# Two score evictions, the state products and the order of transfers in the first chunk of a gated linear attention with a mixture of experts

## The chip, the cores and the metric

The kernel runs on one core of one Trainium2 chip. A core has TensorE (PE in the profile; it multiplies matrices and writes only to PSUM, 8 banks of 128 x 512 float32), VectorE (DVE), ScalarE (ACT), GpSimd (POOL) and SyncE (SP, which here only issues transfers), and 16 DMA engines that all queues share. Each engine works through its own instruction list in order; semaphores order the engines among each other. The metric is device time in microseconds (us), lower is better.

## The reference

There are 4 batches, 8 heads, 768 positions and 48 features a head. A recurrence with a gate for each feature runs over the positions, and its output goes through a mixture of four experts:

```
f = 1 / (1 + exp(-f_logit))
for t in range(S):
    state = f[:, :, t, :, None] * state + einsum('bhd,bhe->bhde', k[:, :, t], v[:, :, t])
    y[:, :, t] = einsum('bhd,bhde->bhe', q[:, :, t], state)

x = y, as (batch * position) x (head * feature)            # 3072 x 384
p = domain_probs / (sum(domain_probs) + 1e-9)
for e in range(4):
    out += p[:, e] * (relu(x @ w1[e]) @ w2[e])             # 384 -> 1024 -> 384
```

## The kernel before

**Chunks.** The 768 positions are cut into 6 chunks of 128. Within a chunk the recurrence becomes matrix products. With g = ln(1 + exp(-f_logit)) (`gate1`, `gate2`, L326 to L336) and its running sum cs, made by a product with a triangle of ones (`pe_cs`), q is multiplied by exp(-cs) and k by exp(cs) (`exps`, `expq`, `product`). Both are transposed (`pe_tp` with TensorE in chunk 0, otherwise by a transfer) into QK, the scores k.q are made (`pe_at`, L430), evicted from PSUM to AT as bfloat16 with a multiplication by a 0/1 triangle, `mask01` (`ev_at`, L433), and multiplied by v (`pe_y`, L444). From the second chunk on, the state of the chunks before is added to y (L440). After a chunk, the state takes up k'v (`pe_kv` on TensorE, L450; `ev_kv` adds it on DVE, L457) and is multiplied by the chunk's total decay (`state` on GpSimd, L462 and L465). y is then copied, transposed (`pe_xt`, L469) and copied again to become x, or is scaled and transposed by a transfer, and goes into the experts.

**Experts.** Chunks 0 and half of chunk 1 run the plain form: `mm_h` (L478) for x @ w1, a relu eviction (L489), `mm_o` (L493) for h @ w2. The rest uses a form with seven instead of eight products for a pair of experts and a pair of tiles, on scaled x: `mm_hs` (L510), relu (L516, L518), sums of blocks (`s_sum`, L528), products `mm_p` (L547) and their additions (`ev_p`, L555).

**Chunk 0.** It comes first, batch by batch (0 to 3), while all data is still on its way. f and q of chunk 0 are loaded so that two neighbouring positions stand together in one partition's run ("paired", `PAIRED = "fq"`, L291), so the running sum for q (`pe_cq`, L356) and the columns of the scores come in an order of pairs that `pe_at` undoes when it reads q: its moving operand is read as position pair by pair, with the two members a long step apart (L428), and the scores stand in the order of positions. `pe_cs` of chunk 0 also makes the total decay: eight matmuls, each with one column of `par` (L349). f, k and q are loaded by SyncE in the order of their due times; v (chunk 0) and the weights are loaded by GpSimd's queue, with a conversion to bfloat16, in the order `SEQ` ("v0 v1 w0 v2 v3 w1") and then w2 to w10. Pieces w0 and w1 are the two halves of expert 0's w1, w2 and w3 those of expert 1's, w4 and w5 the two halves of expert 0's w2; later pieces are whole matrices. `GATE` holds v0's issue until k of batch 1 has landed, and v1's until k of batch 2 has. GpSimd's eight DMA semaphores are reused in turn: an issue waits until the transfer eight issues before has landed.

**The order of the work.** No loop of the text sets the order on the engines. Every step (an `Op`, made by `P.add`) has an estimated cost for each engine that may run it, dependences, buffers that it takes and frees, and a due time ("prio"). `Plan.run` plays the program through: whenever an engine is free, it gets the ready step with the lowest due time. The list of steps in the order of the played time is then emitted, each engine's in that order. `MOVES` holds corrections for single steps: `name=offset` is added to the due time, `@ENGINE` fixes the engine. Names are `kind chunk.batch...`, for example `ev_at0 0.1` (evict scores, head half 0, chunk 0, batch 1), `kv 0.0` (state product), `h 0.0.4.0` (chunk 0, expert 0, blocks 4 to 7 of the hidden layer, columns from 0 on), `ld k0.1` (load). Steps of DMA queues are played with an estimate too, so an offset on "w 0" or "ld v0.0" changes only what the plan believes of the landing. Before the first L478 matmul, gaps that the plan sees on TensorE are filled with matmuls on a constant ("fillers", L925, 128 x 512): one for each 0.42 us before 7 us, and one for each 0.25 us after it (L914).

**State products of chunk 0.** `kv 0.b` depends on y of its batch and on the last x of chunk 0 (L715), so that all four come after the transposes of batch 3.

Of the kernel before, what the change touches and what calls it, by code (L numbers as in the profile page):

```python
# [10 lines left out]
AF = mybir.ActivationFunctionType  # L11
ALU = mybir.AluOpType
# [128 lines left out]
def kernel(  # L141
# [14 lines left out]
    T = 128  # L156
# [181 lines left out]
    def pe_cs(c, b):  # L338
# [8 lines left out]
        for i in range(NP):  # L347
            for j in range(2):
                nc.tensor.matmul(out=cs[:, HD + i:HD + i + 1], lhsT=flat(g, j * 2 + i % 2), rhs=par[:, i // 2:i // 2 + 1],  # L349
                                 start=(j == 0), stop=(j == 1), skip_group_check=True)  # L350
# [16 lines left out]
    def exps(c, b):  # L367
        cs = tl("cs", c, b)
        src = cs[:, 0:HD].rearrange("t (i r d) -> t i r d", r=2, d=D)
        for j in range(2 if c else 0):  # L370
            o, i = e_part(c, b, j), src
            if j == 0:
                o, i = (x.rearrange("t i r d -> t r i d") for x in (o, i))
            nc.scalar.activation(out=o, in_=i, func=AF.Exp, scale=1.0 if j else -1.0)  # L374
        if c == 0:
            nc.scalar.activation(out=tl("e", c, b)[:, 2 * NP * P2:], in_=cs[:, 0:HD], func=AF.Exp, scale=1.0)
            nc.scalar.activation(out=tl("egs", c, b)[0:MP, 0:NP], in_=cs[0:MP, HD:HD + NP], func=AF.Exp, scale=-1.0)
# [7 lines left out]
    def product(c, b, j, eng):  # L385
        if (c, j) == (0, 0):
# [583 lines left out]
```

## Time and profile before

| | us |
|---|---|
| runs shown | 288.28, 289.12, 294.09 (median 289.12) |
| profiled execution, its own time | 287.92 |
| its span, first to last instruction | 286.2 |
| TensorE busy | 279.5 (98%) |
| VectorE busy | 199.8 (70%) |
| ScalarE busy | 177.9 (62%) |
| GpSimd busy | 110.7 (39%) |
| L510 (x @ w1, second form) | 106.8 |
| L547 (products of the second form) | 29.0, 28.4, 28.2 and 14.7 by operands |
| L493 (h @ w2, first form) | 35.0 |
| L478 (x @ w1, first form) | 35.0 |
| L433 (masked score evictions, 48) | 30.4 |

Busy time of a group is the union of its instructions' durations. A matmul's duration includes its passage through the array, so that matmuls overlap, and the distance from start to start is what one costs in a row of them. "Idle before" is the time in which the engine did nothing ahead of an instruction, with what ended it. The granted clock of TensorE is a share of full speed. In the lines of a timeline the first number is the start in us from the first instruction, the second the duration of the run of instructions that the line merges. Data movement is dense over the first 45 us (the page's row of 40 slices shows 6 to 9 tenths there) because the weights are still coming.

### The profile page before, as it was taken

How to read it: one execution, taken by the hardware profiler on the slowest of the kernel's cores; microseconds unless marked ns; L12 is line 12 of the kernel's file. 1: busy time of each engine (PE TensorE's matmuls, PEld its weight loads, DVE VectorE, ACT ScalarE, POOL GpSimd, SP SyncE). 2: the span in 40 equal slices, each digit the busy share in tenths (PEclk: the TensorE clock that was granted, in tenths of full speed). 3: DMA queues.
4: the chain of work that ended last, by engine and by line, in shares of the span. 5: the costliest groups of instructions: out<-in, count | busy, mean ns of one | idle time of the engine just before them, and what ended most of it. 6: DMA issues, size and time to landing. Idle time of an engine off the chain costs nothing.

```text
span 286.2 us, 7542 instructions
## 1 busy us (share of the span) xinstructions
PE 279.5 (98%) x3046; PEld 237.1 (83%) x3046; DVE 199.8 (70%) x397; ACT 177.9 (62%) x334; POOL 110.7 (39%) x183
## 2 busy tenths in 40 slices
PE   5999999999999999999999999999999999999995
PEld 2768555567777999999999999999999999999995
DVE  5675123688889878987789877878682888453374
ACT  5968673558757874953577846649466667255530
POOL 5766501327773752867037276427235000000000
PEclk9999999999999999999999999999999999999999
DMA  6999999996997999899979999789744136110001
GB/s 157 213 193 207 206 192 205 190 187 141 192 166 148 210 140 236 156 168 209 214 141 186 147 212 205 142 176 187 128 55 82 30 76 123 57 60 0 30 27 57
DMA packets 153687, 41.87 MB, mean 146 GB/s; under 512 B 144028, under 2 KB 152860, under 8 KB 153652
## 3 DMA queue, kind: packets, MB, share of 16 engines
q1 hardware_dynamic: 142404, 34.66, 62.9%
q0 software_dynamic: 11248, 6.72, 16.6%
q8 instruction: 24, 0.39, 0.6%
q14 instruction: 11, 0.09, 0.1%
HBM read 31.51 MB, written 4.72 MB: 127 GB/s over the span
## 4 chain that ended last, share of the span: by engine, by line
PE 94%; SPq 2%; DMA 1%; DVE 1%; ACT 1%; issue 0%; DVEq 0%
PE ps_m L510 33%; PE ps_m L547 29%; PE ps_m L493 11%; PE ps_m L478 11%; PE ps_m L430 3%; PE ps_m L444 2%; SPq L293 1%; PE ps_m L440 1%; DMA q<-in_q_dram 1%; PE ps_m L450 1%; PE ps_m L341 1%; SPq L295 1%; PE ps_m L399 1%; PE ps_m L925 0%; DVE qk L387 0%; PE ps_m L469 0%
## 5 line engine op out<-in xcount | busy, mean ns | idle before, releaser
L510 PE MATMUL ps_m<-x,w_sb 128*128 128x256 bf16 x864 | 106.8, 273 | 0.0
L518 ACT ACTIVATE h<-ps_m 128x512 bf16<-128x512 f32 x108 | 64.3, 597 | 48.6 <-PE ps_m L510 37.8
L510 PEld LDWEIGHTS <-w_sb 128*128 128x128 bf16 x864 | 82.7, 98 | 9.2
L547 PEld LDWEIGHTS <-S 128*128 128x128 bf16 x576 | 48.8, 98 | 1.2 <-issue 0.2
L555 DVE TENSOR_TENSOR o<-ps_m,o 128x192 f32<-128x192 f32 x91 | 30.8, 352 | 23.8 <-PE ps_m L547 22.7
L547 PEld LDWEIGHTS <-h 128*128 128x128 bf16 x432 | 36.4, 98 | 0.7
L465 POOL TENSOR_TENSOR Sf<-Sf,egs 48x192 f32<-48x192 f32 x40 | 21.5, 540 | 36.1 <-DVE Sf L457 27.7
L493 PE MATMUL ps_m<-w_sb,h 128*128 128x384 bf16 x192 | 35.0, 326 | 0.0
L478 PE MATMUL ps_m<-x,w_sb 128*128 128x128 bf16 (+2 forms) x264 | 35.0, 282 | 0.0
L528 DVE TENSOR_TENSOR S<-h 128x1024 bf16<-128x1024 bf16 x36 | 28.1, 792 | 8.0 <-ACT h L518 7.9
L489 ACT ACTIVATE h<-ps_m 128x512 bf16<-128x512 f32 (+1 forms) x50 | 24.7, 508 | 13.6 <-PE ps_m L478 12.6
L433 DVE TENSOR_TENSOR AT<-ps_m,mask 128x512 bf16<-128x512 f32 x48 | 30.4, 682 | 2.7 <-PE ps_m L430 2.7
L516 DVE TENSOR_SCALAR h<-ps_m 128x512 bf16<-128x512 f32 x36 | 24.6, 688 | 10.6 <-PE ps_m L510 8.4
L478 PEld LDWEIGHTS <-w_sb 128*128 128x128 bf16 x264 | 21.8, 98 | 9.4
L413 ACT ACTIVATE yb<-ps_m,pn 128x384 bf16<-128x384 f32 x48 | 25.9, 580 | 5.6 <-PE ps_m L444 2.5
L547 PE MATMUL ps_m<-ts_sb,S 128*128 128x192 bf16 x288 | 29.0, 246 | 0.0
L547 PE MATMUL ps_m<-w_sb,S 128*128 128x192 bf16 x288 | 28.4, 246 | 0.0
L390 POOL TENSOR_TENSOR qk<-q,e 128x384 bf16<-128x384 f32 x18 | 22.4, 1251 | 15.2 <-ACT e L374 14.3
L374 ACT ACTIVATE e<-ps_m 128x384 f32<-128x384 f32 x40 | 23.1, 704 | 8.2 <-PE ps_m L341 7.2
L547 PE MATMUL ps_m<-w_sb,h 128*128 128x192 bf16 x288 | 28.2, 246 | 0.0
L493 PEld LDWEIGHTS <-h 128*128 128x128 bf16 x192 | 18.3, 98 | 11.7
L390 POOL TENSOR_TENSOR qk<-k,e 128x384 bf16<-128x384 f32 x18 | 17.9, 999 | 11.6 <-PE ps_m L444 3.6
(83 smaller groups left out, 314.9 us busy)
## 6 DMA issues: line engine op xcount, KB each, us to landing
out_dram<-o SPq DMA_DIRECT2D x23, 192.0 KB, 2.2
w_sb<-in_moe_w_dram POOLq DMA_DIRECT2D x5, 768.0 KB, 17.0
k<-in_k_dram SPq DMA_DIRECT2D x10, 384.0 KB, 4.9
q<-in_q_dram SPq DMA_DIRECT2D x10, 384.0 KB, 5.6
v<-in_v_dram SPq DMA_DIRECT2D x10, 384.0 KB, 4.5
f<-in_f_logit_dram SPq DMA_DIRECT2D x9, 384.0 KB, 5.2
w_sb<-in_moe_w_dram POOLq DMA_DIRECT2D x6, 384.0 KB, 10.1
f<-in_f_logit_dram SPq DMA_DIRECT2D x6, 192.0 KB, 3.8
```

Of the source, the lines that this page charges most:

```text
L390: return engines[eng].tensor_tensor(out=tl("qk", c, b)[:, j, :, 0:D].rearrange("t (i r) d -> t i r d", r=2), in0=tl("qk"[j], c, b // 2)[:, ...
L413: nc.scalar.activation(out=ys, in_=y, func=AF.Copy, scale=pe)
L433: nc.vector.tensor_tensor(out=tl("AT", c, b)[:, r].rearrange("s i t -> s (i t)"), in0=tl("A", c, b, r).rearrange("s i t -> s (i t)"), in1= ...
L478: nc.tensor.matmul(out=hp(c, e, fc, n0, n1, nf)[:, f], lhsT=w1_sb[:, e, kk, (fc + f) * 128:(fc + f + 1) * 128], rhs=tl("xT", c)[:, kk, n0: ...
L489: nc.scalar.activation(out=dst, in_=src, func=AF.Relu)
L493: nc.tensor.matmul(out=tl("op", c, e, nt, part)[:, cols], lhsT=tl("h", c, e, half_of(c, nt * T))[:, fc, nt * T:(nt + 1) * T], rhs=w2_sb[:, ...
L510: nc.tensor.matmul(out=out_[:, f], lhsT=w1_sb[:, e, kk, (fc + f) * 128:(fc + f + 1) * 128], rhs=tl("xs", c, hf, p)[:, el, kk, :], start=(k ...
L516: nc.vector.tensor_relu(out=dst, in_=tl("hp", c, hf, p, el, fc))
L518: nc.scalar.activation(out=dst, in_=tl("hp", c, hf, p, el, fc), func=AF.Relu)
L528: return nc.vector.tensor_tensor(out=s(j), in0=in0, in1=in1, op=op)
L547: nc.tensor.matmul(out=out_, lhsT=lhs[:, fc, :], rhs=rhs[:, fc, :], start=(first and fc == 0), stop=(fc == KF - 1), skip_group_check=True)
L555: nc.vector.tensor_tensor(out=o, in0=src, in1=o, op=ALU.add)
```

## The change

In chunk 0:

- For `BYPOOL = "1.1 2.1"`, that is head half 1 of batches 1 and 2, the masked eviction on DVE is replaced by a plain copy on ScalarE and then a select on GpSimd that sets the upper triangle to zero in place (`mask_at`).
- `pe_at` reads q with the pairs inside (a step of two positions) and the two members outside, so the scores stand in PSUM in the paired order; the evictions put them back in the order of positions.
- The total decay comes from four matmuls with both columns of `par` instead of eight with one.
- `kv 0.b` no longer waits for the last x.
- `SEQ` becomes "v0 v1 v2 w0 v3 w1"; the due times of the loads change, so that f0 f1 k1 f2 come first; the planned landings of v and of w0 and w1 get other due times (`VW`).
- All four batches' products with q and k may be run by DVE or GpSimd, also batch 3's.
- Fillers after 7 us are issued only for a planned gap of over 1.2 us (`PADGAP`), one for each 0.25 us beyond 0.5.
- `MOVES` is another list, for all chunks: 25 lines before, 22 after.

The parts for an unpaired q (`"q" in PAIRED` false) are not used, since `PAIRED` stays "fq". The diff, with the two lists cut to the entries of the first chunk and a few more:

```diff
 MOVES = (
-    "ld k0.0=1.3;ld f0.1=-1.7;ld k0.1=-2.4;ld f0.2=-4.6;ld f0.3=-2.2;ld k0.2=-5.4;ld q0.2=-2.1;w 0=3;w 5=-3.6;ld k1.2=5.8;"
-    "ev_tp 0.0=17.3@ACT;tpq 0.2=25.4;q 0.3=-16.4;ld p=-2.3;v 1.0=-49@POOL;v 1.1=0@POOL;egs 1.3=3.1;ev_kv 1.1=22.8;ev_kv 1.3=37.7;"
...
+    "ld f0.0=-58.8;ld f0.1=-61.7;ld k0.1=-53.8;ld f0.2=-42.3;ld k0.2=-2.1;ld v0.0=1520.4;w 0=-1521;ld v0.3=-2.1;w 5=-34.9;"
+    "gate1 0.2=-7.8;cs 0.0=-2.4;expq 0.1=40.3;cs 0.1=-2.2;exps 0.1=-7;q 0.2=-0.1@DVE;ev_tp 0.3=196.8;ev_at0 0.0=17.1;ev_at1 0.0=13.1;"
+    "ev_y 0.0=5.6;ev_at0 0.1=201.7;kv 0.0=-185.8;ld p=23.8;ev_tp 1.1=11.6@DVE;ev_y 1.1=-9.1;ev_ys 1.2.0.0=31.4@ACT;ev_ys 1.2.0.1=0@ACT;"
+    "ld v2.2=16.8;h 0.0.4.0=27.1;h 0.0.4.128=38.5;h 0.0.4.256=24.1;o 0.2.0.1=1.7;h 0.3.2.0=11;h 0.3.4.0=12.2;h 0.3.6.0=-9.4;"
...
 )
@@ pe_cs
-        for i in range(NP):
+        for i in range(2):
             for j in range(2):
-                nc.tensor.matmul(out=cs[:, HD + i:HD + i + 1], lhsT=flat(g, j * 2 + i % 2), rhs=par[:, i // 2:i // 2 + 1],
+                nc.tensor.matmul(out=cs[:, HD + i:HD + NP:2], lhsT=flat(g, j * 2 + i), rhs=par,
                                  start=(j == 0), stop=(j == 1), skip_group_check=True)
@@ pe_at
-                if c == 0:
-                    qt = QK[rows, 0].rearrange("m (j i) (p g) -> m i g p j", i=2, g=2)[:, i % 2, i // 2]
-                    a = a.rearrange("t (p j) -> t p j", j=2)
+                if c == 0 and "q" in PAIRED:
+                    qt = QK[rows, 0].rearrange("m (j i) (p g) -> m i g p j", i=2, g=2)[:, i % 2, i // 2].rearrange("m p j -> m j p")
+                    a = a.rearrange("t (j p) -> t j p", j=2)
                 nc.tensor.matmul(out=a, lhsT=QK[rows, 1, i, :], rhs=qt, start=True, stop=True)
 
-    def ev_at(c, b, r):
+    def mask_at(c, b, r):
+        a = tl("AT", c, b)[:, r]
+        nc.gpsimd.affine_select(out=a, in_=a, compare_op=ALU.is_ge, fill=0.0, base=0, channel_multiplier=-1, pattern=[[0, NP], [1, T]])
+
+    def ev_at(c, b, r, eng):
+        if eng == "ACT":
+            nc.scalar.copy(out=tl("AT", c, b)[:, r].rearrange("s i (p j) -> s i j p", j=2),
+                           in_=tl("A", c, b, r).rearrange("s i (j p) -> s i j p", j=2))
+            return
+        if c == 0 and "q" in PAIRED:
+            nc.vector.tensor_tensor(out=tl("AT", c, b)[:, r].rearrange("s i (p j) -> s i j p", j=2),
+                                    in0=tl("A", c, b, r).rearrange("s i (j p) -> s i j p", j=2),
+                                    in1=mask01.rearrange("s (i p j) -> s i j p", j=2, i=NP), op=ALU.mult)
+            return
         nc.vector.tensor_tensor(out=tl("AT", c, b)[:, r].rearrange("s i t -> s (i t)"),
                                 in0=tl("A", c, b, r).rearrange("s i t -> s (i t)"), in1=mask01, op=ALU.mult)
@@ the plan's steps
-            pe = {"DVE": 0.47} if c == 0 and b == B - 1 else {"DVE": 0.47, "POOL": 1.36} if c == 0 else None
+            pe = {"DVE": 0.47, "POOL": 1.36} if c == 0 else None
...
-            at = P.add(f"at {c}.{bs[-1]}", {"PE": 0.43 if len(bs) == 1 else 0.66}, lambda e, bs=bs: [pe_at(c, b) for b in bs], slot(bs[-1], 7),
+            at = P.add(f"at {c}.{bs[-1]}", {"PE": 0.5 if c == 0 and "q" in PAIRED else 0.43 if len(bs) == 1 else 0.66}, lambda e, bs=bs: [pe_at(c, b) for b in bs], slot(bs[-1], 7),
...
-            eA = [P.add(f"ev_at{r} {c}.{b}", {"DVE": 0.685}, on(ev_at, r), s(7) + 0.1 + 0.1 * r, deps=[at],
+            eA = [P.add(f"ev_at{r} {c}.{b}", {"ACT": 0.6} if c == 0 and f"{b}.{r}" in BYPOOL.split() else {"DVE": 0.685}, one(ev_at, r), s(7) + 0.1 + 0.1 * r, deps=[at],
                         takes=[("AT", c, b)], frees=[pt_("A", r)]) for r in range(2)]
+            for r in range(2):
+                if c == 0 and f"{b}.{r}" in BYPOOL.split():
+                    eA[r] = P.add(f"mask{r} {c}.{b}", {"POOL": 0.65}, on(mask_at, r), s(7) + 0.2 + 0.1 * r, deps=[eA[r]])
...
-            kv = P.add(f"kv {c}.{b}", {"PE": 0.22}, on(pe_kv), s15, deps=[Y[b]] + (X[B - 1] if c == 0 else []),
+            kv = P.add(f"kv {c}.{b}", {"PE": 0.22}, on(pe_kv), s15, deps=[Y[b]],
                        takes=[pt_("KV")], frees=[("vb", c, b), ("qk", c, b)], lag=0.2)
@@ after the plan
-            o.pad, t = int((o.start - t) / (0.42 if t < 7.0 else 0.25)), o.end
+            gap = o.start - t
+            o.pad, t = int(gap / 0.42) if t < 7.0 else int((gap - 0.5) / 0.25) if gap > PADGAP else 0, o.end
@@ constants
+PADGAP = 1.2
-SEQ = "v0 v1 w0 v2 v3 w1"
+SEQ = "v0 v1 v2 w0 v3 w1"
+BYPOOL = "1.1 2.1"
+VW = (-2000, -480)
```

More of the change, by code (lines that the diff above doesn't have):

```diff
@@ L369, in exps @@
         src = cs[:, 0:HD].rearrange("t (i r d) -> t i r d", r=2, d=D)
-        for j in range(2 if c else 0):
+        for j in range(0 if c == 0 and "q" in PAIRED else 2):
             o, i = e_part(c, b, j), src
-            if j == 0:
+            if j == 0 and c > 0:
                 o, i = (x.rearrange("t i r d -> t r i d") for x in (o, i))
             nc.scalar.activation(out=o, in_=i, func=AF.Exp, scale=1.0 if j else -1.0)
+        if c == 0 and "q" in PAIRED:
+            nc.scalar.activation(out=tl("e", c, b)[:, 2 * NP * P2:], in_=cs[:, 0:HD], func=AF.Exp, scale=1.0)
         if c == 0:
-            nc.scalar.activation(out=tl("e", c, b)[:, 2 * NP * P2:], in_=cs[:, 0:HD], func=AF.Exp, scale=1.0)
             nc.scalar.activation(out=tl("egs", c, b)[0:MP, 0:NP], in_=cs[0:MP, HD:HD + NP], func=AF.Exp, scale=-1.0)
@@ L385, in product @@
     def product(c, b, j, eng):
-        if (c, j) == (0, 0):
+        if (c, j) == (0, 0) and "q" in PAIRED:
             return engines[eng].tensor_tensor(out=tl("qk", c, b)[:, 0, :, 0:D].rearrange("t (j h) d -> t j h d", j=2),
@@ L426, in pe_at @@
                 qt, a = QK[rows, 0, i, :], tl("A", c, b, r)[:, i, :]
-                if c == 0:
-                    qt = QK[rows, 0].rearrange("m (j i) (p g) -> m i g p j", i=2, g=2)[:, i % 2, i // 2]
-                    a = a.rearrange("t (p j) -> t p j", j=2)
+                if c == 0 and "q" in PAIRED:
+                    qt = QK[rows, 0].rearrange("m (j i) (p g) -> m i g p j", i=2, g=2)[:, i % 2, i // 2].rearrange("m p j -> m j p")
+                    a = a.rearrange("t (j p) -> t j p", j=2)
                 nc.tensor.matmul(out=a, lhsT=QK[rows, 1, i, :], rhs=qt, start=True, stop=True)
-    def ev_at(c, b, r):
+    def mask_at(c, b, r):
[6 more added lines that the diff above has]
+            return
+        if c == 0 and "q" in PAIRED:
+            nc.vector.tensor_tensor(out=tl("AT", c, b)[:, r].rearrange("s i (p j) -> s i j p", j=2),
+                                    in0=tl("A", c, b, r).rearrange("s i (j p) -> s i j p", j=2),
+                                    in1=mask01.rearrange("s (i p j) -> s i j p", j=2, i=NP), op=ALU.mult)
+            return
         nc.vector.tensor_tensor(out=tl("AT", c, b)[:, r].rearrange("s i t -> s (i t)"),
@@ L589 @@
                                 deps=issued[-1:] + gate(x), takes=[("vb", 0, i)], lag=1.2))
-            ld[0, "v", i] = P.add(f"ld v0.{i}", {"DMA": 1.1}, lambda _: None, -480 + j, deps=issued[-1:], lag=2.0)
+            ld[0, "v", i] = P.add(f"ld v0.{i}", {"DMA": 1.1}, lambda _: None, VW[0] + j, deps=issued[-1:], lag=2.0)
             continue
@@ L599 @@
                     -600 + 2 * j, deps=issued[-1:] + gate(x) + ([ld[1, "k", 0]] if i == w_last else []))
-        op = P.add(f"w {i}", {"DMA": 2.05 if i < 6 else 4.4}, lambda _: None, -400 if i == w_last else -480 + j, deps=[iss], lag=1.0)
+        op = P.add(f"w {i}", {"DMA": 2.05 if i < 6 else 4.4}, lambda _: None, -400 if i == w_last else (VW[1] if i < 2 else -480) + j, deps=[iss], lag=1.0)
         issued.append(iss)
@@ L628, in attention @@
             eq = []
-            if c == 0:
+            if c == 0 and "q" in PAIRED:
                 cq = P.add(f"cq {c}.{b}", {"PE": 0.4}, lambda e, b=b: pe_cq(b), s(0) - 0.1,
@@ L635, in attention @@
                        deps=[G[b]], takes=[pt_("cs")], lag=0.2, frees=[("gp", c, half)])
-            ex = P.add(f"exps {c}.{b}", {"ACT": 1.2 if c else 0.6}, on(exps), s(0) + 0.1, deps=[cs],
+            ex = P.add(f"exps {c}.{b}", {"ACT": 1.2 if c else 0.6 if "q" in PAIRED else 0.94}, on(exps), s(0) + 0.1, deps=[cs],
                        takes=[("e", c, b)] + ([("egs", c, b)] if c == 0 else []), frees=[pt_("cs")])
```

41 rows, old and new, of the table MOVES are left out of this document.

## The prediction

> **What bounds the kernel now.** I first read the windows: busy time by stretch, with the number of instructions and the granted clock.
>
> ```profile
> core 0: us, PE busy (x) PEld busy (x) DVE busy (x) ACT busy (x) POOL busy (x), PEclk, DMA share, GB/s
> 0.00:20.00 20.00, 16.58 (x189) 10.58 (x190) 12.87 (x29) 14.64 (x31) 13.19 (x29) 1.00 1.20 186
> 20.00:30.00 10.00, 10.00 (x141) 7.99 (x139) 5.80 (x18) 7.78 (x15) 7.26 (x14) 1.00 1.24 207
> ...
> 50.00:90.00 40.00, 40.00 (x368) 27.84 (x368) 32.62 (x61) 27.10 (x54) 21.43 (x35) 1.00 0.97 170
> 90.00:130.00 40.00, 40.00 (x472) 37.05 (x467) 33.73 (x65) 26.84 (x49) 22.59 (x35) 1.00 0.99 182
> ```
>
> From 20 us on TensorE has no idle time in any stretch until its last matmul (282.9 us in the chain); DVE, the next, reaches 33.73 of 40. A busy TensorE need not be at its best, so I also looked at the distance from each matmul's start to the next: it is the same for every shape from 20 us to the end (109 ns for 256 columns, 163 for 384), except some 0.2 us around each group of L430. So the time is the start of the first L478 matmul, plus a fixed pile of TensorE work, plus 3.3 us of last addition and store. Only two things can be gained: an earlier start, or work taken out of the pile. A loss can also come from holes in the pile, which has none now. The timeline of TensorE shows the start:
>
> ```profile
> 17.00 0.60 PE L925 MATMUL ps_m<-S 128*128 128x512 bf16 x2
> 17.48 0.34 PE L469 MATMUL ps_m<-ident,yb 128*128 128x128 bf16 x3
> 17.66 0.36 PE L444 MATMUL ps_m<-vb,AT 128*128 128x48 bf16 x8
> 17.97 0.72 PE L430 MATMUL ps_m<-QK 48*128 48x128 bf16 x8
> 18.62 0.39 PE L925 MATMUL ps_m<-S 128*128 128x512 bf16 x1
> 18.84 0.36 PE L444 MATMUL ps_m<-vb,AT 128*128 128x48 bf16 x8
> 19.05 0.33 PE L469 MATMUL ps_m<-ident,yb 128*128 128x128 bf16 x3
> 19.21 0.59 PE L925 MATMUL ps_m<-S 128*128 128x512 bf16 x2
> 19.64 0.83 PE L478 MATMUL ps_m<-x,w_sb 128*128 128x128 bf16 x12
> ```
>
> The first L478 starts at 19.64 us. Its weights, w0, landed at 18.52 us (end of that transfer in the trace) and its x was copied by 18.34 (ScalarE, 17.86 + 0.48). So neither holds it: what stands ahead of it in TensorE's order does. That is y of batch 2 (L444 at 18.84), which waits for the fourth of a row of score evictions on DVE, and five fillers (L925). The evictions and the copies around them:
>
> ```profile
> 13.94 1.02 ACT L281 COPY QK<-ps_m 112x1024 bf16<-112x1024 bf16 x1
> 16.46 0.59 ACT L281 COPY QK<-ps_m 112x512 bf16<-112x512 bf16 x1 [1.51 <-PE ps_m L399]
> ```
> ```profile
> 15.89 2.51 DVE L433 TENSOR_TENSOR AT<-ps_m,mask 128x512 bf16<-128x512 f32 x4
> ```
>
> DVE evicts batches 1 and 2 in one run to 18.40; ScalarE has 1.51 us free just before 16.46.
>
> **The change, part by part.**
>
> *Two evictions leave DVE.* DVE loses 2 x 0.64 us (2.51 / 4 each). ScalarE gets two copies of 128x512 from PSUM, 0.60 us each by the L518 row (597 ns); a permuted form costs little (L333, permuted, 521 ns; L376, not, 493 for 384 columns). GpSimd gets two selects of 0.64 us (the select that builds the mask, L216, 637 ns). The first copy fits into the 1.51 us. The second falls at about 17.1, where ScalarE is full, and delays its neighbours by at most 0.6; DVE, now lighter, can take some of them. For one half, the chain is 0.60 + 0.64 plus a hand-over, longer than the 0.64 it replaces, but it runs beside the other half. The remaining masked evictions read and write in another order; bounds are 0 (L387 and L390 have different permutations, both 557 ns) and 0.1 us each (the spread of the L433 rows, doubled); I take 0. What matters is y of batch 2: ready at 18.4 before, and about 18.4 after (scores ready 17.0, copy to 17.7, select to 18.35). So this part brings nothing there; it brings y of batch 1 forward, from 17.66 to about 17.0.
>
> *Fillers.* After 7 us a filler is now issued only for planned gaps over 1.2 us. Of the fillers shown, five lie between 17.0 and the start: 0.48 + 0.22 + 0.43 = 1.13 us of TensorE's order. They are not all gain, since the waits beneath stay: y of batch 2 could start at about 18.6 and the transpose behind it at 18.8, so the first L478 could start at about 19.0 instead of 19.64.
>
> *Order of transfers.* v2 now goes ahead of w0 on GpSimd's queue, so w0 lands later. In the trace w0 landed at 18.52, v2 at 18.70 and v3 at 19.30, so one v is about 0.6 us, and w0 should land between 18.70 (both were there by then) and 19.12. v1's issue waits for k2, now the eighth load instead of the seventh, hence 0.8 us later (landings 9.19 and 10.02); GpSimd's queue still has work until 12.5, so that is hidden. w1 (21.17) has the same transfers ahead of it and stays. Three of the four L478 groups that need w1 are put far back, so it has slack. I put the first L478 at 19.05, **0.6 us earlier**, with 18.7 and 19.64 as bounds. [...]
>
> *State products early.* All four of L450's groups now run inside the pile:
>
> ```profile
> 23.53 0.50 PE L450 MATMUL ps_m<-vb,qk 128*128 128x96 bf16 x8
> ...
> 24.54 0.33 PE L450 MATMUL ps_m<-vb,qk 128*128 128x96 bf16 x4
> ...
> 26.05 0.33 PE L450 MATMUL ps_m<-vb,qk 128*128 128x96 bf16 x4
> ```
>
> Sixteen matmuls, 42 ns apart: 0.67 us. The wait for the last x goes, and each is bound to its own y. Batch 0 has a large offset forward; its y is done at 16.2, so it surely moves into idle time. Batch 1 probably follows, 2 and 3 have their y too late. Two of four, **0.34 us**; bounds 0.17 and 0.67. Their additions on DVE and GpSimd come earlier, where DVE has just lost 1.28 us.
>
> *Total decay by two columns.* Four matmuls instead of eight per batch, 25 ns apart: 0.1 us each, inside the head where TensorE waits anyway. I take 0; at most 0.1 (last batch, at 13.1).
>
> *Scores.* The moving operand is read in another order, same columns: 0.65 us a group now (16.36 to 17.00), later chunks 0.55 to 0.6. I take 0; bounds -0.1 and +0.1 a batch, mostly under waits.
>
> *Offsets from chunk 1 on.* They reorder TensorE, ScalarE and DVE through the whole pile but add no instruction. They cannot gain, since nothing is idle; they can only open holes. DVE at 82 to 84% leaves some 6 us in each 40, so small delays are absorbed. I take 0, with 3 us as the bound from the nearest row, the largest wait that TensorE shows before 20 us (1.5 us), twice.
>
> **Sum.** 0.6 + 0.34 = 0.94 us. The profiled execution took 287.92 us (span 286.2 and 1.7 around it), so its like would take 287.0. The runs shown are 288.28, 289.12 and 294.09; the profiled one lies 1.2 below their median, and the middle of the three undisturbed times (287.92, 288.28, 289.12) is 288.28. Forecast: 288.28 - 0.9 = **287.4 us**.
>
> **The rivals.**
>
> *A. GpSimd's order makes it slower.* Its row in the trace:
>
> ```profile
> 12.88 3.79 POOL L306 DMA_DIRECT2D w_sb<-in_moe_w_dram  x5
> 18.80 2.40 POOL L306 DMA_DIRECT2D w_sb<-in_moe_w_dram  x3 [2.13 <-DMA w_sb<-in_moe_w_dram]
> ```
>
> The seventh weight issue stands 2.13 us until w0 has landed, because it reuses w0's semaphore. In the new order this wait falls on the eighth weight issue, reached at about 18.3. The second select becomes due at 17.7. If it stands behind that issue, it starts at 19.1 + 0.75 = 19.9 and ends at 20.5, against 18.40 for the eviction it replaces: y of batch 2 is 2.1 us late. If the first L478 comes behind that y, its start is 20.8 instead of 19.64, and the sum is +1.2 - 0.34 = +0.9: **289.1 us, slower**. It decides at one point: whether the select is queued before or behind that issue, and y ahead of the first L478. Against it: some 0.6 us of room. 12%.
>
> *B. Holes in the pile.* The new order makes TensorE wait for evictions or x in later chunks, 1 to 3 us in all: 287.4 + 2 = **289.4**. For it: several hundred instructions change place. Against it: DVE's room. 20%.
>
> *C. The head does not move.* w0 lands late enough (19.6 or later) or the last batch's chain (q3 lands last, at 14.85) holds x. Then only L450 remains, eaten by one wait: **288.3**. 10%.
>
> *D. The clock.* Six fillers at the start have their weight loads 0.43 us apart (1.92, 2.35, 2.78, 3.20); those at 17 us run 0.22 apart. So TensorE starts at half speed and is at full speed from about 4.2 us on. With fewer fillers it might fall back. At the start it took 2.7 us of work (1.5 to 4.2) to come up; if the first L478 had to do that again at half speed, 1.35 us would be lost: 287.4 + 1.35 = **288.8**. The trace's only fall comes 4.6 us after the last matmul (at 287.5 against 282.9), and the new rule leaves no planned gap beyond 1.2 us unfilled. 3%. [...]
>
> **How the numbers follow.** The forecast holds 55% (286.4 to 288.2: start at 18.7 or 19.64, L450 0.17 or 0.67). A, B, C and D hold 45%. The low end takes both best bounds, 0.94 + 0.67 + 0.1 = 1.7 from 288.28, and 0.9 more for the spread between runs: 285.7. The high end is B's 289.4 plus the other 1 us of its bound: 290.4. A measurement of this kernel can tell about 2% (5.8 us) from no change. Faster by that would need six times the sum: 1%. Slower by that needs holes of 6.7 us, more than twice B's bound: 4%. Within 2%: 95%.
>
> **What would show it.** First L478 at 19.0 to 19.1 and no filler just ahead of it: that step is right. At 19.6: C; at 20.5 or later with a select after 19.5: A. Two groups of L450 ahead of the first L478: that term is right. Starts of matmuls farther apart than their shape's 109, 163 or 83 ns after 30 us: B. Weight loads 0.43 us apart at the first L478: D. The prediction is wrong if these holes exceed the 0.9 us that the head gives.

## The result, and the profile after

| | before | changed |
|---|---|---|
| median, us | 288.82 (288.06 to 294.09, 21 runs) | 287.67 (286.48 to 289.17, 21 runs) |
| profiled execution, us | 287.92 | 286.64 |
| its span | 286.2 | 284.9 |
| first x @ w1 product starts | 19.64 | 19.09 |
| from there to the start of the last matmul (the pile) | 263.02 | 261.98 |
| from the last matmul's end to the end of the span (the tail) | 3.30 | 3.60 |

The ratio is 0.9958, with an interval of 0.9939 to 0.9977: about 1.2 us less. That is clear of the noise, but far under the 2% (5.8 us) from which a kernel is called faster. Ratios here are taken over fast runs (none over 1.5% above the fastest of its kernel), so they need not be the quotient of the medians. The forecast was 287.4. In the profiled execution, 0.55 us come from the start and 1.04 from the pile, and 0.3 go back in the tail.

First the windows of the changed kernel. Their columns are the same as before.

```profile
core 0: us, PE busy (x) PEld busy (x) DVE busy (x) ACT busy (x) POOL busy (x), PEclk, DMA share, GB/s
0.00:20.00 20.00, 15.26 (x184) 11.18 (x185) 14.87 (x36) 13.56 (x31) 14.44 (x31) 1.00 1.23 187
20.00:30.00 10.00, 10.00 (x123) 7.44 (x121) 4.27 (x12) 8.58 (x15) 9.39 (x18) 1.00 1.24 207
...
50.00:90.00 40.00, 40.00 (x379) 28.38 (x378) 32.77 (x62) 28.41 (x57) 21.14 (x35) 1.00 0.96 170
90.00:130.00 40.00, 40.00 (x460) 37.07 (x459) 34.08 (x64) 25.91 (x48) 23.59 (x35) 1.00 0.99 192
```

TensorE is still full from 20 us on, and the distances from start to start are the same as before (109, 163 and 82 ns by shape): no holes have come in, and two have gone (below). Before 20 us it is now less busy, 15.26 against 16.58, because 20 fillers have become 6, all of them at the very start. Its timeline (start, duration, line and tiles of each run of instructions) shows the new head:

```profile
14.74 0.41 PE L428 MATMUL ps_m<-QK 48*128 48x128 bf16 x8 [1.02 <-DVE QK L279]
...
17.48 0.33 PE L461 MATMUL ps_m<-vb,qk 128*128 128x96 bf16 x4
17.66 0.55 PE L455 MATMUL ps_m<-vb,AT 128*128 128x48 bf16 x8
18.05 0.33 PE L461 MATMUL ps_m<-vb,qk 128*128 128x96 bf16 x4
18.22 0.33 PE L480 MATMUL ps_m<-ident,yb 128*128 128x128 bf16 x3
18.48 0.40 PE L428 MATMUL ps_m<-QK 48*128 48x128 bf16 x8
18.93 0.33 PE L480 MATMUL ps_m<-ident,yb 128*128 128x128 bf16 x3
19.09 2.17 PE L489 MATMUL ps_m<-x,w_sb 128*128 128x128 bf16 x36
```

The lines have moved: L489 was L478, L455 was L444 (y), L461 was L450 (state products), L480 was L469. Three things are to be seen. The scores of batch 2 are made at 14.74 instead of 16.36. Its y stands at 17.66 instead of 18.84. From 17.48 on TensorE goes from one group into the next with short waits only, 0.4 us in all by the distances from start to start, so the first product at 19.09 waits for little but the work ahead of it. The longest of them, 0.18 us, lies inside y of batch 2: its first matmul starts at 17.66, the other seven from 17.86 on, behind the select that ends at 17.81. And three of the four state products are now in this head (two are shown, the other stands at 15.52). The two moved evictions, on ScalarE and on GpSimd:

```profile
12.32 0.72 ACT L436 CAST AT<-ps_m 128x512 bf16<-128x512 f32 x1
...
15.49 0.74 ACT L436 CAST AT<-ps_m 128x512 bf16<-128x512 f32 x1 [1.17 <-PE ps_m L455]
```
```profile
14.45 1.19 POOL L432 TENSOR_SCALAR_AFFINE_SELECT AT<-AT 128x512 bf16<-128x512 bf16 x1
15.60 1.55 POOL L303 DMA_DIRECT2D w_sb<-in_moe_w_dram  x2
17.16 0.65 POOL L432 TENSOR_SCALAR_AFFINE_SELECT AT<-AT 128x512 bf16<-128x512 bf16 x1
```

The copies took 0.72 and 0.74 us, against 0.60 in my sum. The selects took 1.19 and 0.65. No weight issue waits for a landing in this trace, so rival A did not happen in its size. A small form of it did: the second copy ended at 16.23 (15.49 + 0.74), but its select began only at 17.16, behind two weight issues on GpSimd.

In the pile, 12 state-product matmuls less are 0.51 us, and three transposes less 0.17. The rest, 0.36 us, is two gaps. In both traces TensorE loses some 0.22 us around every group of scores (95 ns ahead of it, 120 behind). Before, there were 11 such places from chunk 1 on; now there are 10, because two groups that stood apart (57.9 and 59.5 us) run as one. And a gap of 0.14 us behind a running sum, at 163.5 us before, is gone.

### The profile page after: what moved, and what is told of

Same layout as the page of the kernel before. It is cut to its first block, busy times and chain, and to the rows that moved or that the text cites. A ratio compares the mean times of both kernels' runs of the same rounds, so it can differ in the third digit from the quotient of the medians.

```text
span 284.9 us, 7480 instructions
## 1 busy us (share of the span) xinstructions
PE 276.6 (97%) x3016; PEld 236.3 (83%) x3016; DVE 195.9 (69%) x394; ACT 178.3 (63%) x339; POOL 111.2 (39%) x183
## 4 chain that ended last, share of the span: by engine, by line
PE 93%; SPq 2%; DMA 2%; DVE 1%; ACT 1%; issue 0%; DVEq 0%
PE ps_m L521 33%; PE ps_m L558 29%; PE ps_m L504 11%; PE ps_m L489 11%; PE ps_m L428 2%; PE ps_m L455 2%; DMA q<-in_q_dram 2%; SPq L290 2%; PE ps_m L451 1%; PE ps_m L461 1%; PE ps_m L338 1%; SPq L292 1%; PE ps_m L397 0%; PE ps_m L480 0%; DVE AT L440 0%
## 5 line engine op out<-in xcount | busy, mean ns | idle before, releaser
L529 ACT ACTIVATE h<-ps_m 128x512 bf16<-128x512 f32 x114 | 67.6, 597 | 63.4 <-PE ps_m L521 44.2
L504 PE MATMUL ps_m<-w_sb,h 128*128 128x384 bf16 x192 | 36.0, 326 | 0.0
L489 PE MATMUL ps_m<-x,w_sb 128*128 128x128 bf16 (+2 forms) x264 | 35.8, 282 | 0.0
L539 DVE TENSOR_TENSOR S<-h 128x1024 bf16<-128x1024 bf16 x36 | 25.6, 735 | 9.0 <-ACT h L529 8.9
L500 ACT ACTIVATE h<-ps_m 128x512 bf16<-128x512 f32 (+1 forms) x47 | 24.0, 519 | 11.8 <-PE ps_m L489 10.4
L444 DVE TENSOR_TENSOR AT<-ps_m,mask 128x512 bf16<-128x512 f32 x40 | 25.4, 682 | 5.3 <-PE ps_m L428 5.3
L504 PEld LDWEIGHTS <-h 128*128 128x128 bf16 x192 | 18.4, 98 | 12.4
L489 PEld LDWEIGHTS <-w_sb 128*128 128x128 bf16 x264 | 21.6, 98 | 8.3
L527 DVE TENSOR_SCALAR h<-ps_m 128x512 bf16<-128x512 f32 x30 | 20.4, 690 | 10.2 <-PE ps_m L521 8.6
L388 POOL TENSOR_TENSOR qk<-k,e 128x384 bf16<-128x384 f32 x18 | 19.2, 1073 | 12.5 <-PE ps_m L461 3.5
L411 ACT ACTIVATE yb<-ps_m,pn 128x384 bf16<-128x384 f32 x43 | 22.8, 581 | 1.3 <-PE ps_m L455 0.7
```

The source lines that it names most:

```text
L388: return engines[eng].tensor_tensor(out=tl("qk", c, b)[:, j, :, 0:D].rearrange("t (i r) d -> t i r d", r=2), in0=tl("qk"[j], c, b // 2)[:, ...
L411: nc.scalar.activation(out=ys, in_=y, func=AF.Copy, scale=pe)
L444: nc.vector.tensor_tensor(out=tl("AT", c, b)[:, r].rearrange("s i t -> s (i t)"), in0=tl("A", c, b, r).rearrange("s i t -> s (i t)"), in1= ...
L489: nc.tensor.matmul(out=hp(c, e, fc, n0, n1, nf)[:, f], lhsT=w1_sb[:, e, kk, (fc + f) * 128:(fc + f + 1) * 128], rhs=tl("xT", c)[:, kk, n0: ...
L500: nc.scalar.activation(out=dst, in_=src, func=AF.Relu)
L504: nc.tensor.matmul(out=tl("op", c, e, nt, part)[:, cols], lhsT=tl("h", c, e, half_of(c, nt * T))[:, fc, nt * T:(nt + 1) * T], rhs=w2_sb[:, ...
```

## The experiments

All times are medians with their spread. They were measured in three groups, e1 to e4, e5 to e8 and e9 to e12, the last on another chip than the first two, each beside runs of the kernel before. Those of them that kept full clock have medians of 288.51, 288.26 and 288.46, so the groups can be compared to about 0.25 us; e9 to e12 are read against e6. "Start" is that of the first x @ w1 product in the profiled execution.

### e1 and e2: both kernels once more

No edit. These two give the level of the first chip.

> The kernel before, unchanged, to see its granted clock run by run. Its profiled execution is at full speed from 4.2 us on, that of the changed kernel from 9.0 us on, and the changed kernel's runs spread from 286.5 to 289.2 us with mean clocks between 0.988 and 1.0. Theory F (the fillers hold the clock): the mean clock here is 0.998 to 1.0 in nearly all runs, and the undisturbed times lie within 1 us of each other (288.1 to 289.1). Rival G (the clock varies by itself, whatever the kernel does at its start): mean clocks here spread as widely, down to 0.988, and so do the times.

> The changed kernel, unchanged, beside its variants on the same chip. Expected 0.9958 of the kernel before (0.994 to 0.998), first L489 at 19.1 us; theory F: mean clocks between 0.988 and 1.0 from run to run, and time falls with the clock by about 1.7 us for 0.012.

Before: 288.26 (287.76 to 292.17). Changed: 288.21 (286.56 to 288.93), ratio 0.9947 (0.9913 to 0.9982) against the 35 further runs of the kernel before beside e1 to e4 (median 288.90). The medians of e1 and e2 are as good as equal, and the spread says why once the runs are sorted by their mean granted clock. It does not vary smoothly, but by steps:

| mean granted clock | changed, first measurement | changed, e2 | before, beside e1 to e4 |
|---|---|---|---|
| 0.998 to 1.0 | 9 runs, 286.48 to 287.98 | 4 runs, 286.56 to 288.49 | 20 runs, 287.77 to 289.59 |
| 0.992 to 0.994 | 8 runs, 287.38 to 288.18 | 4 runs, 287.65 to 288.36 | 7 runs, 290.02 to 292.29 |
| 0.987 to 0.988 | 4 runs, 288.46 to 289.17 | 4 runs, 288.49 to 288.93 | 5 runs, 291.57 to 292.46 |
| 0.982 to 0.983 | none | none | 3 runs, 293.02 to 294.83 |

At full clock the changed kernel lies at about 286.8, the one before at about 288.4: 1.6 us apart. But in 12 of the changed kernel's 21 runs TensorE lost some of its clock: by the medians of the rows, one step cost it 1.1 to 1.2 us and two 1.7 to 2.0. That was rival D in its effect, to which I had given 3%; where in the run the clock fell is not known for the changed kernel, since both of its profiles kept it. The kernel before loses its clock too (15 of 35 runs here, and 2 of the 12 of e1), so rival G, that the clock varies whatever the fillers, holds in part for it. And it loses more by each step: 3.1 us for the first, by the medians of the rows. By an estimate from the length of e5's fall (3.41 us at half speed, see the last section), one such window costs a busy TensorE at most 0.5 x 3.41 = 1.7 us, so something else must go with it there; no such run was profiled, and this stays open.

### e3 and e4: the fillers alone

e3 gives the changed kernel the old filler rule, e4 gives the kernel before the new one:

```diff
 e3
-            gap = o.start - t
-            o.pad, t = int(gap / 0.42) if t < 7.0 else int((gap - 0.5) / 0.25) if gap > PADGAP else 0, o.end
+            o.pad, t = int((o.start - t) / (0.42 if t < 7.0 else 0.25)), o.end
 e4
-            o.pad, t = int((o.start - t) / (0.42 if t < 7.0 else 0.25)), o.end
+            gap = o.start - t
+            o.pad, t = int(gap / 0.42) if t < 7.0 else int((gap - 0.5) / 0.25) if gap > PADGAP else 0, o.end
```

> The changed kernel with the old rule for fillers: 11 more fillers between 8 and 15 us, everything else in the same order. Theory F: the clock is 0.998 to 1.0 in nearly all runs, the spread falls under 1 us and the median to 286.5 to 287.0, about 0.7 us below the changed kernel (0.992 to 0.994 of the kernel before). The prediction's step (fillers stand in the way of the first product): the first product starts 0.2 to 0.6 us later than 19.1 us, and the median is 0 to 0.5 us above the changed kernel's.

> The kernel before with the new rule for fillers only: 13 fewer fillers. The prediction's step: the first L478 starts at about 19.0 to 19.3 us instead of 19.64, and the profiled time falls by 0.4 to 0.6 us if the clock is full. Theory F: the start may move as much, but the mean clock falls below 0.998 in many runs, so that the median of the times is not below the kernel before (ratio 0.998 to 1.003), with a spread of 2 us.

e3 took 287.37 (286.93 to 287.64), ratio 0.9906 (0.9871 to 0.994). Its start is later, 19.95 (0.75 to 0.86 us later than the changed kernel's, where 0.2 to 0.6 was expected), 0.5 us more in the median than the changed kernel at full clock, and yet it is the steadier: none of its 12 runs lost clock. e4 took 289.92 (287.46 to 293.0), ratio 1.0004 (0.9959 to 1.0049). Its start came 0.54 us earlier than in the kernel before, as the step on the fillers had it:

```profile
18.71 0.37 PE L444 MATMUL ps_m<-vb,AT 128*128 128x48 bf16 x8
18.93 0.33 PE L469 MATMUL ps_m<-ident,yb 128*128 128x128 bf16 x3
19.10 0.83 PE L478 MATMUL ps_m<-x,w_sb 128*128 128x128 bf16 x12
```

But 9 of its 12 runs lost clock, down to 0.977. So in these runs the fillers do two things: they stand in the way of the first product (19.64 or 19.50 in e1 against 19.10; 19.95 against 19.09 or 19.20 in e2: 0.4 to 0.9 us), and they hold the clock (lost in none of 12 runs of e3 against 12 of 21 and 8 of 12 of the changed kernel, and in 15 of 35 and 2 of 12 runs of the kernel before against 9 of 12 of e4). Taking out fillers alone brought no gain that could be measured.

### e5 and e6: which fillers hold the clock

Both are the changed kernel with a fixed table of fillers, put where TensorE waits anyway. e6 has a few more than e5, spread over the stretch from 7 to 17 us:

```diff
+    FILL = {'cs 0.0': 7, 'at 0.1': 1, 'at 0.2': 4, 'tpk 0.3': 1}                                                # e5
+    FILL = {'cs 0.0': 7, 'tpk 0.0': 1, 'at 0.0': 1, 'at 0.1': 1, 'cq 0.3': 1, 'at 0.2': 4, 'tpk 0.3': 2}   # e6
+    for o in done:
+        o.pad = FILL.get(o.name, 0)
```

> The changed kernel with fillers only where its trace shows TensorE waiting: a seventh at the start (0.78 us idle before the first sums), one before the scores of batch 1 (0.45 to 0.5 us idle), four before those of batch 2 (1.02 idle) and one before the last transpose of batch 3 (0.35 idle). Theory F: the first product stays at 19.0 to 19.3 us, the mean clock is 0.998 or more in most runs, and the median falls to 286.6 to 287.2 us, below both the changed kernel and its variant with the old rule (287.37). Rival H (only fillers that are dense enough before 12 us hold the clock): the clock still falls to 0.988 to 0.994 in half of the runs, median 287.5 to 288.2.

> As the run before, with four more: one before the first transpose, one before the scores of batch 0, one before the running sum of batch 3, and a second before the last transpose. Theory F: the clock is full in nearly all runs, the first product 0.2 to 0.4 us later than in the run before (those at half speed are 0.43 us long and nothing waits there), median 286.8 to 287.3. Rival H: only this one of the two holds the clock.

e6 took **286.91** (286.58 to 287.45) and kept its clock in all 6 runs; its ratio is 0.9875 (0.9816 to 0.9933), the lowest of all, though against runs of the kernel before that had lost clock more often than elsewhere (their median is 290.69). e5 took 287.15 (286.58 to 288.85), with two of 6 runs one step down. One of those was profiled. Its windows, then those of e6 in the same stretches:

```profile
6.50:13.30 6.80, 4.20 (x61) 3.23 (x61) 4.05 (x8) 4.16 (x12) 2.81 (x4) 1.00 1.17 222
13.40:16.70 3.30, 3.22 (x20) 2.12 (x19) 3.30 (x7) 1.70 (x5) 3.30 (x5) 0.50 1.57 119
16.80:30.00 13.20, 12.56 (x197) 10.40 (x199) 7.11 (x20) 10.52 (x21) 12.03 (x23) 1.00 1.32 199
```
```profile
6.50:13.30 6.80, 5.19 (x72) 3.68 (x71) 4.65 (x9) 4.82 (x12) 3.01 (x5) 1.00 1.37 227
13.40:16.70 3.30, 3.16 (x47) 2.22 (x45) 3.30 (x7) 1.96 (x6) 3.29 (x5) 1.00 1.58 152
16.80:30.00 13.20, 13.03 (x178) 9.98 (x176) 7.42 (x20) 11.29 (x21) 12.55 (x23) 1.00 1.32 203
```

In e5 the granted clock is 0.50 from 13.36 to 16.77 us; TensorE gets 20 instructions through in that window, e6 47. Two lines of e5's timeline, the idle time ahead of the fall and a row of fillers within it:

```profile
13.48 0.80 PE L353 MATMUL ps_m<-gp,Wp 128*128 128x192 bf16 x4 [1.14 <-ACT gp L330]
...
15.29 1.74 PE L943 MATMUL ps_m<-S 128*128 128x512 bf16 x4
```

The longest gap ahead of the fall is 1.14 us, shorter than the 1.2 us that I had named as harmless. e5 is busy for 4.20 of the 6.80 us before (and only half of the 3.41 us just before), e6 for 5.19. That the busy share as such decides is not shown: the last section has windows with less of it than e7's that held.

### e7 and e8: order of transfers and evictions, first try

e7 puts the issue of w0 back ahead of that of v2. e8 has DVE do all evictions of chunk 0, with the masked multiplication in the new order:

```diff
 e7
+    at = {o.name: i for i, o in enumerate(done)}
+    i, j = at["v issue 2"], at["w issue 0"]
+    done[i], done[j] = done[j], done[i]
 e8, mask_at
+        return
 e8, ev_at
-        if eng == "ACT":
-            nc.scalar.copy(out=tl("AT", c, b)[:, r].rearrange("s i (p j) -> s i j p", j=2),
-                           in_=tl("A", c, b, r).rearrange("s i (j p) -> s i j p", j=2))
-            return
```

> The changed kernel with v2 and w0 issued in the old order, all else in place. Theory V (y of batch 2 needs v2, which lands at 17.3 to 18.7 us in the old order, against 16.0 now): y of batch 2 starts at 17.9 to 18.8 instead of 17.66, and the first product at 19.4 to 20.1; time at full clock 286.9 to 287.6. The prediction's step (v2 ahead of w0 only delays w0, which lands at 16.6 to 18.5 in the old order): the first product stays at 19.1 or starts earlier, time at full clock 286.3 to 286.7.

> The changed kernel with the two evictions back on DVE, in the places of the two copies in the order, and no selects. The prediction's step (this part brings nothing for y of batch 2): the first product at 19.0 to 19.3 us, time at full clock 286.4 to 286.9. Theory D (DVE is the engine that the head's chain goes through, some 0.7 us idle between 11.5 and 17.5 us, and 1.4 us comes back): y of batch 2 0.5 to 1.2 us later, the first product at 19.6 to 20.3, time at full clock 287.1 to 287.8.

e7 took 287.97 (286.97 to 289.79), with start 20.37. e8 took 288.04 (287.52 to 289.56), with start 21.36. Both profiled executions had lost two windows of clock in the head (6.83 us at half speed), and no run of e8 kept its clock. e7's two runs at full clock, 287.09 and 287.83, lie 0.3 and 1.0 above the changed kernel's 286.83. At the same clock step e8 takes no more than the changed kernel (287.74 against 287.9); why the evictions seem to cost nothing there is not shown. So these two were inconclusive on the price of either part, and both were repeated on e6's fillers, where the clock holds.

### e9: all evictions on DVE, with steady clock

The edit of e8 together with that of e6; the rival to the prediction's "brings nothing".

> The changed kernel with the fillers of e6 (clock full; median 286.91, first product 19.28 us, y of batch 2 at 17.85) and all evictions on DVE, no copies and selects. The prediction's step (this part brings nothing for y of batch 2): the first product at 19.1 to 19.5 us, median 286.7 to 287.1. Theory D (it shortens DVE's chain): y of batch 2 at 18.6 to 19.2, the first product at 20.0 to 20.6, median 287.6 to 288.2.

288.28 (287.79 to 289.27), ratio 0.9967 (0.9936 to 0.9998): **1.37 us more than e6**, most of the 1.6 us that the change is worth at full clock. All runs kept their clock. First DVE's timeline, then TensorE's, then TensorE's in e6:

```profile
17.23 1.33 DVE L437 TENSOR_TENSOR AT<-ps_m,mask 128x512 bf16<-128x512 f32 x2
18.46 0.72 DVE L465 TENSOR_TENSOR Sf<-Sf,ps_m 48x192 f32<-48x192 f32 x2
19.21 0.42 DVE L279 COPY QK<-ps_m 112x512 bf16<-112x512 bf16 x1
```
```profile
18.64 0.36 PE L452 MATMUL ps_m<-vb,AT 128*128 128x48 bf16 x8
...
19.69 0.40 PE L428 MATMUL ps_m<-QK 48*128 48x128 bf16 x8
20.55 0.33 PE L477 MATMUL ps_m<-ident,yb 128*128 128x128 bf16 x3 [0.45 <-DVE Sf L465]
20.71 1.00 PE L486 MATMUL ps_m<-x,w_sb 128*128 128x128 bf16 x15
```
```profile
14.94 0.40 PE L428 MATMUL ps_m<-QK 48*128 48x128 bf16 x8
...
17.85 0.56 PE L455 MATMUL ps_m<-vb,AT 128*128 128x48 bf16 x8
...
18.68 0.40 PE L428 MATMUL ps_m<-QK 48*128 48x128 bf16 x8
19.12 0.33 PE L480 MATMUL ps_m<-ident,yb 128*128 128x128 bf16 x3
19.28 2.17 PE L489 MATMUL ps_m<-x,w_sb 128*128 128x128 bf16 x36
```

With two more evictions DVE ends those of batch 2 at 18.56 (17.23 + 1.33), so y stands at 18.64 instead of e6's 17.85 (of which all but the first matmul runs from 18.06). Behind them come the state additions and the last copy of QK (to 19.63, in e6 to 18.20), on which batch 3's scores wait; those run at 19.69 instead of 18.68. The start goes from 19.28 to 20.71.

Of these 1.43 us, 0.26 are not the evictions': DVE's product with q of batch 2, which waits for q to land, starts at 12.76 here and at 12.50 in e6. The other 1.17 are: the scores of batch 2 follow that product by 3.05 us instead of 2.44, and the start follows those scores by 4.90 instead of 4.34. The second distance is a good measure, since it is 4.34 or 4.35 us in the profiles of the changed kernel, e2, e3, e5, e6 and e12. So the price is 1.2 us by the trace and 1.4 by the medians. e8 speaks for less: with one window of clock lost its median is 287.74, only 0.9 above the changed kernel at full clock. And the price is that of an order that was planned without these two evictions on DVE; no run plans it anew with them.

### e10: the state products of the head twice

e6 with every state-product matmul of batches 0 to 2 in chunk 0 issued twice in place: twelve more matmuls, 0.50 us of TensorE work. One theory has idle time under them, the other has TensorE full there.

```diff
-        for i in range(NP):
+        for i in [i for i in range(NP) for _ in range(2 if c == 0 and b < 3 else 1)]:
```

> The fillers of e6, and the twelve early matmuls of the state products (batches 0 to 2) issued twice, 0.50 us more of TensorE's work ahead of the first product. If early state products lie in idle time, as the prediction has it, the first product stays at 19.2 to 19.4 us and the median at 286.8 to 287.1. Rival: TensorE is already full from 17.3 us on, so that what is put there moves the first product: two of the three groups lie behind 17.3, so +0.34, the first product at 19.6, median 287.2.

287.18 (286.83 to 287.56), ratio 0.993 (0.9903 to 0.9957): 0.27 more than e6, which is near what the groups can be compared to. The start, 19.72, is 0.44 later. TensorE's timeline:

```profile
15.24 0.40 PE L428 MATMUL ps_m<-QK 48*128 48x128 bf16 x8
...
18.07 0.50 PE L461 MATMUL ps_m<-vb,qk 128*128 128x96 bf16 x8
18.41 0.36 PE L455 MATMUL ps_m<-vb,AT 128*128 128x48 bf16 x8
18.61 0.50 PE L461 MATMUL ps_m<-vb,qk 128*128 128x96 bf16 x8
```

Each group is lengthened by 0.17. But the scores of batch 2, which stand ahead of all three, already come 0.30 later here (15.24 against 14.94), again with the landing of q. From those scores to the start it is 4.49 us against 4.34: 0.15 us is the doubled products', and the rest of their 0.50 us fell into short waits, such as the one inside y of batch 2, which has none here. So of the 0.5 us that the state products freed in the pile, 0.15 by the trace (0.27 by the medians) would have come back at the start: what they bring is 0.2 to 0.4 us, and most of it is idle time that they fill, as the prediction had it.

### e11: w0 ahead of v2, with steady clock

The edits of e7 and e6 together.

> The fillers of e6, with v2 and w0 issued in the old order. Theory V: y of batch 2 waits for v2 until 17.3 to 18.7 us, the first product at 19.4 to 20.1, median 287.1 to 287.7. The prediction's step: nothing is late but w0, which lands earlier: first product at 19.3 or before, median 286.6 to 286.9.

287.84 (287.11 to 289.13), ratio 0.9956 (0.993 to 0.9982): **0.93 more than e6**, start 20.07 against 19.28. TensorE's timeline, then the view of its waits from 14 to 21 us (line, releaser, total, times, longest):

```profile
18.93 0.36 PE L455 MATMUL ps_m<-vb,AT 128*128 128x48 bf16 x8 [1.02 <-DMA vb<-in_v_dram]
```
```profile
PE ps_m L455 <- DMA vb<-in_v_dram: 1.0, 1, 1.0
```

In the old order v2 lands at 18.89, and the y of batch 2, whose scores are ready by then, waits 1.02 us for it. From the scores of batch 2 to the start it is 5.24 us against 4.34, so the trace gives 0.90. The landing of v2 varies from execution to execution in the old order (17.33 in e4, 18.18 in e1, 18.45 in e7, 18.70 before, 18.89 here); in the new one it was at 15.97 in the changed kernel and at 15.3 to 15.6 in e2, e3, e6, e9, e10 and e12.

### e12: the end of the old order

e6 with six of the old order's entries for the last chunk put at the end of `MOVES`:

```diff
+    "hs 5.0.1.0.6=-10.3;p 5.0.1.7=12;hs 5.1.0.1.4=36.3;hs 5.1.1.1.2=8.3;s3 5.1.1=8.3;s4 5.1.1=52.5"
```

> The fillers of e6, and for the last chunk the six offsets of the kernel before, which put the product with one addition behind it last, in place of the one with two. The time from the last matmul's end to the end of the span is 3.6 us in every run of the changed kernel and 3.3 in the kernel before. If the order of the last two products makes this, it falls to 3.3 here and the median to 286.6; rival: the stores make it, and it stays at 3.6 and 286.9.

286.66 (286.18 to 288.03), ratio 0.9928 (0.9894 to 0.9962). The tail is the old one again, 3.23 against 3.60, so those entries set it: in the changed kernel the last product has two additions behind it, before it had one. But the pile grew by 0.39 (262.37 against 261.98: two more gaps of 0.2 us, one between products with w2 at 29.6 us, one behind a score group at 58.3), and the spans are alike (285.17, 285.11). The runs lie in two clusters, seven up to 286.88 and four from 287.61 on, and what parts them stays open. It is not told apart from e6.

## Why the prediction was right in its sum, and where its steps were wrong

**What held.** The bound was right: a start, a pile without holes, a tail. The start was put at 19.05 and came at 19.09; the sum was 0.94 and the profiled executions differ by 1.28, the medians by 1.15. The fillers' share of the start stands by e4 (0.54). w0 landed at 18.68 and held nothing up, though the new order delays it by more than my 0.2 to 0.6 us: over the profiles it lands at 18.5 on average, against 17.1 in the old order. Total decay and the offsets from chunk 1 on opened no hole. Rivals B and C did not come about, and A only in the small form above.

**"This part brings nothing there" was wrong.** e9 puts the two evictions' move at 1.2 to 1.4 us. I had reckoned that y of batch 2 would still be ready at about 18.4, from scores at 17.0, a time that I took over from the trace of before. But what leaves DVE there also brings forward what stands behind it, QK of batch 2 first: its scores were made at 14.74, and the same chain of copy and select ended at 17.81. In e9 they are made at 15.81, so not all of the way from 16.36 is the evictions'. An engine's order must be played forward, not only the one instruction shortened.

**Order of transfers: counted as a cost, was a gain.** e11 puts it at 0.9 us. The trace of before had it in view: y of batch 2 at 18.84 had two late inputs, DVE's eviction at 18.40 and v2's landing at 18.70. I named the first and used the second only to price w0. Both inputs had to come earlier, which fits with their prices (1.2 to 1.4 and 0.9) adding to more than the 1.6 us that the whole is worth at full clock; no run gives one of the two parts alone to the kernel before.

**Where their gain went.** e4, the kernel before without the late fillers, starts at 19.10, and the changed kernel at 19.09. So beyond the fillers the other parts did not bring the start forward. They made room ahead of the same start for three groups of state products and three more transposes of x, 0.68 us of work that e4 still does in the pile.

**State products: the size held, with another count.** Three groups moved, not two, and freed 0.51 us in the pile; 0.15 to 0.27 of it comes back at the start (e10). That leaves 0.2 to 0.4 against my 0.34.

**Terms put at nothing.** "They cannot gain, since nothing is idle", said of the offsets from chunk 1 on, was wrong: I had seen the 0.2 us around each score group and not counted that the new order has one such place less, and one other gap less, 0.36 us together. The transposes of x that move ahead of the start, 0.17, were not in the sum. The scores of chunk 0 were put at 0 with a bound of 0.1: a group now takes 0.34 us from its first matmul to the next step, against 0.65, with waits around it.

**Tail.** The 0.3 us there were not in the sum; I had not looked at the order of the last chunk, though `MOVES` was replaced for all chunks.

**Rival D was given too small a chance.** I put the price at 1.35 us; one step costs 1.1 to 1.2. That they are close is in part luck, for I had thought of a fall at the first product itself, and in the profiled falls (e5, e7, e8) it came ahead of it, at 13.4 to 17.4 us. "No planned gap beyond 1.2 us unfilled" was the wrong measure (e5: a fall with no gap over 1.14). In 12 of the 21 runs it happened. It lifts the changed kernel's median from about 286.8 to 287.67.

So the sum came out near because missed gains (evictions, order, the two gaps) were offset by missed losses (clock, tail) and by the fact that the parts overlap; that part of it is luck. e6 keeps the change and puts fillers where TensorE waits: at 286.91 it is the best of them, 0.76 below the changed kernel's first median and 1.3 below its second, by keeping the clock; at full clock the two are alike (286.8 and 286.9).

**Not tested.** No run puts the loads of f, k and q back in their old order. They matter in the head: q of batch 1 lands at 9.07 us instead of 10.76, and the scores of batch 1 are made at 11.14 instead of 14.22, in e9 too (11.13), so this is not the evictions' doing.

## What to carry to other kernels

Where an instruction waits, list all its inputs with the time that each was ready: taking away the last one gains only as far as the next. Taking a load off an engine moves everything behind it, so follow what the next instructions on that engine release. When one execution is compared with another, measure from an event that comes behind the same landings (here the scores of batch 2), or the landings' own spread is read as a price. Filler matmuls belong into the waits of a sparse stretch (spread from 7 to 17 us they kept the clock in all 6 runs of e6, the fewer of e5 in 4 of 6), and not ahead of the work that ends the stretch (0.4 to 0.9 us of the start, e3 and e4); look at the spread of many runs and at the granted clock before judging a change of 1 us.

## What the runs showed of the hardware

**The clock changed by whole windows of 3.413 us.** In the records of the granted clock, stretches at half speed ahead of the last matmul lasted 3.413 us (e5) and 6.827 us (e7, e8), one and two windows; the one stretch at full clock lasted 283.306 us in the kernel before and 276.480 in the changed one, 83 and 81 windows. One such window in a run of about 283 us lowers the mean clock by 0.5 x 3.41 / 283 = 0.006, which is the step of the table (1.0, 0.994, 0.988, 0.982). The first rise to full speed came anywhere from 4.2 to 10.9 us (e2), in the kernel before at 4.2 and, unchanged (e1), at 8.6. In the 3.41 us ahead of a fall TensorE was busy for 49% (e5), 39% (e8) and 70% (e7) of the time, with no gap over 1.14 us in e5 and 1.63 in e8. Neither the gaps nor this share part these windows from those that held: counted in steps of 3.413 us from the first rise, windows of 55% (before, from 4.22 us), 57% (e8, from 4.84, with a gap of 1.15 us) and 61% (e9, from 4.68) were followed by full speed. Without the transposes (the matmuls with `ident`) the three falls do come lowest, at 27% (e5), 31% (e8) and 41.5% (e7); the lowest that held have 42.2% (e4, from 10.16 us), 45% (e2, from 14.30) and 46% (e12, from 7.59). That is an order seen afterwards in 14 traces with three falls, not a threshold.

**A select on GpSimd took longer beside a product on DVE.** The select of 128x512 took 0.63 to 0.66 us where DVE ran no product of two SBUF operands beside it, and 0.71 to 1.37 in the seven traces where one lay over its time (changed kernel, e2, e5, e6, e7, e11, e12). In all seven the select ended 0.49 us after the product, whenever it had begun itself. The 1.19 above ran from 14.45 to 15.64; DVE's product in the changed kernel's timeline ended at 15.15:

```profile
14.60 0.55 DVE L385 TENSOR_TENSOR qk<-q,e 128x384 bf16<-128x384 f32 x1
```

The product kept its 0.55 us. In e10 the product began only 0.11 us before the select's end, and neither was lengthened. In the changed kernel, e2, e7 and e11 the select is recorded as the first to start (starts on GpSimd are rough in these records), and it was the one that got longer. Why it got longer is not shown.
